# Output projection of an attention block: earlier loads of some heads, and modulation sums moved behind other products

## The chip, the cores and the metric

The kernel runs on one core of one Trainium2 chip. The metric is the time of one execution on the device, in microseconds (us). One execution is also recorded by the hardware profiler; its record is called the trace, and the summary of it the page. All numbers below come from such traces or from timed runs. Two numbers of different sharpness are used: the time of the whole, which differs by 2 us and more from run to run, and the length of one stage in a trace, which repeats to 0.2 us in the kernel before (two traces).

## The reference, cut to what matters

```python
mod = (silu(c) @ w_mod).reshape(1, 6, 1, -1)
sa, ca, ga, sb, cb, gb = mod[:, 0], ..., mod[:, 5]
h = layernorm(x) * (1 + ca) + sa
x = x + ga * attention(h, k_cache, v_cache, wq, wo)      # ends in: concat(heads) @ wo
h = layernorm(x) * (1 + cb) + sb                         # needs sb, cb
x = x + gb * gmlp(h, w_in, w_sp, b_sp, w_out)
```

There are 2048 tokens, width 1024 and 32 heads of 128. The stage in question is `concat(heads) @ wo`, a product of 2048 x 4096 by 4096 x 1024. While it runs, the kernel also computes `sb` and `cb`, which the next layer norm needs: 16 columns of 128 values, each a weighted sum of a slice of `w_mod` with `silu(c)`. These are the modulation sums.

## The kernel before

The projection is cut into eight blocks of 256 tokens. Each block does a 2 x 2 matrix product with seven products in place of eight (the Strassen and Winograd way). A product is 16 matmuls of 128 x 128 by 128 x 512. The price of the saved product is operand sums, which VectorE (DVE) makes: `o_sum`.

Blocks overlap. In the steady state the order of the products is 1 and 2 of block n, 3 of block n-1, 6 and 7 of block n, 4 of block n-1, 5 of block n, and then block n+1. What has to happen behind a product hangs on it as a hook. Reading a finished product out of TensorE's result memory and adding it to x is called its evacuation. In the timelines below, DVE and the queue of loads work through their instructions in the order of the program: the modulation sum at 1246.34 us holds up the evacuation behind it, and a store at 1287.7 us the loads behind it.

```python
SPOTS = ((2, 1), (2, 2), (1, 4), (2, 6), (2, 7), (3, 1), ...)   # (block, product); 28 of them
mod_at = {}
for q in range(16):
    k = q * 8 // 5
    mod_at.setdefault(SPOTS[k + 3], []).insert(0, lambda q=q: mod_sum(q))
    mod_at.setdefault(SPOTS[k], []).append(lambda q=q: load_mod(q))
...
def load_mod(q):                       # a transposing load, 256 KB, two buffers
    t = wm_t[q] = mods.tile([P, D], BF16, name="wm_t", tag="wm_t", bufs=2)
    nc.sync.dma_start(out=t[:], in_=w_mod[:, 3*D + P*q : 3*D + P*(q + 1)], transpose=True)

def load_heads(n, k):                  # block n; pair k=0 feeds products 1 and 7, k=1 feeds 2 and 4
    for q in (2 * k, 2 * k + 1):
        t = oq[n, q] = heap.take("oq", [P, 8, 256], BF16)
        nc.sync.dma_start(t[:, :m, :], oT_dram[8*q : 8*q + m, :, n*256 : (n + 1)*256]...)
...
    for n in range(3, 8):              # the hooks of blocks 3 to 7
        hk = wos[n].hooks
        hk[1] = [o_sum(n, 1), o_sum(n, 3)]     # (lambdas left out)
        hk[2] = [o_sum(n, 2)]                  # product 6 reads this one
        hk[6] = [o_sum(n, 4), ...]             # and product 5 o_sum 1
        ...
        if 4 <= n and n < 8:
            wos[n - 1].on(3 if n < 6 else 4, lambda n=n: n < 7 and load_heads(n + 1, 1))
...
def row_done(ti):                      # both halves of 128 rows of x are finished
    nc.sync.dma_start(x1_dram[ti], x1[:])      # a store that waits for DVE's last add
```

All loads and stores stand in one queue, that of SyncE, in program order. `heap.take` hands out slots of 4 KB per partition, the one that has been free for longest first; a load into a slot waits until the slot's last reader is done.

The softmax here doesn't subtract the row's maximum and nothing guards it: scores larger than these inputs give would overflow.

## Time and profile before

| | before |
|---|---|
| time | 1757.7 us, median of 3 runs (1757.69 to 1757.94) |
| span in the trace | 1754.6 us |
| TensorE (PE) busy | 1734.4 us, 99% |
| DVE busy | 1522.0 us, 87% |
| start of the projection in the trace | 1128.66 us |
| start of the next stage | 1314.33 us |
| **length of the projection** | **185.67 us** |

The two lines of the page that give the busy times of the engines:

```profile
span 1754.6 us, 23657 instructions
PE 1734.4 (99%) x8414; PEld 794.2 (45%) x8414; DVE 1522.0 (87%) x2324; ACT 1298.3 (74%) x1530; POOL 34.1 (2%) x39
```

TensorE is the bound: nothing but its pauses can be won. The Trainium skill (Perfetto Trace Analysis, "Optimization Strategy") advises just that: find the gaps between the slices of the engine that bounds, and what each waits for. The view of waits, for TensorE from 1128 to 1319 us, has three lines (total us, times, longest us):

```profile
PE a L995 <- DVE s_slots L1065: 0.4, 1, 0.4
PE a L995 <- DVE h_slots L1065: 0.3, 1, 0.3
PE c L995 <- DMA wq_t<-oT_dram: 0.3, 1, 0.3
```

This view counts the time between the drawn end of one matmul and the start of the next, and leaves out short ones. The timeline shows more. Its columns are start, duration from first start to last end, engine, line, operation, tiles, shape, number of instructions merged, and in brackets the idle time before with its cause. Here are TensorE's rows of the kernel before: the start of the projection, block 2 (products 1 and 2), block 5 (the second half of product 3 of block 4, then product 6), block 7 (product 1, the halves of product 2, the second half of product 3 of block 6, product 6) and the first row of the next stage:

```profile
1128.66 1.89 PE L995 MATMUL c<-tx,h_slots 128*128 128x512 bf16 x8
...
1170.31 3.62 PE L995 MATMUL a<-wo,oq 128*128 128x512 bf16 x16
1173.92 1.90 PE L995 MATMUL c<-tx,s_slots 128*128 128x512 bf16 x8
1175.75 1.90 PE L995 MATMUL c<-s_slots,oq 128*128 128x512 bf16 x8
...
1248.28 1.89 PE L995 MATMUL a<-s_slots,oq 128*128 128x512 bf16 x8
1250.48 2.76 PE L995 MATMUL a<-h_slots 128*128 128x512 f16 x12 [0.31 <-DVE h_slots L1065]
...
1288.78 3.62 PE L995 MATMUL a<-wo,oq 128*128 128x512 bf16 x16
1292.51 1.90 PE L995 MATMUL c<-tx,h_slots 128*128 128x512 bf16 x8
1294.72 1.90 PE L995 MATMUL c<-s_slots,wq_t 128*128 128x512 bf16 x8 [0.31 <-DMA wq_t<-oT_dram]
...
1298.19 1.89 PE L995 MATMUL a<-s_slots,h_slots 128*128 128x512 bf16 x8
1300.51 2.76 PE L995 MATMUL a<-h_slots,s_slots 128*128 128x512 f16 x12 [0.43 <-DVE s_slots L1065]
...
1314.33 1.49 PE L995 MATMUL a<-h_slots 128*128 128x448 bf16 x7
```

Eight matmuls at full pace take 1.73 us, sixteen take 3.46 us.

What DVE did before product 6 of block 5, in the timeline of the kernel before (L1067 is `o_sum` 3, L933 the modulation sum, L1043 to L1117 the evacuation of product 2, L1065 `o_sum` 2):

```profile
1245.74 0.69 DVE L1067 TENSOR_TENSOR wq_t<-wq_t 128x1024 f16<-128x1024 bf16 x1
1246.34 1.22 DVE L933 SCALAR_TENSOR_TENSOR wm_t<-wm_t,silu_bc 128x1024 bf16<-128x1024 bf16 x1
...
1247.68 0.69 DVE L1043 TENSOR_TENSOR sum<-c,snap 128x512 f32<-128x512 f32 x1
...
1249.74 0.68 DVE L1065 TENSOR_TENSOR h_slots<-os_12192,h_slots 128x1024 f16<-128x1024 f16 x1
```

The modulation sum at 1246.34 stands between the operand sums and the evacuation of product 2, which TensorE had finished before 1247.

The queue of loads and stores around block 7's second head pair (L1084 is the store of x1, L681 a head load; the 11.16 us are two stores merged, the second issued at the end of it):

```profile
1274.62 1.60 SPq L1090 DMA_DIRECT2D h_dram<-hb  x1
1276.86 11.16 SPq L1084 DMA_DIRECT2D x_dram<-x_in  x2
1288.11 0.39 SPq L681 DMA_DIRECT2D h_slots<-oT_dram  x1
1288.59 0.63 SPq L681 DMA_DIRECT2D wq_t<-oT_dram  x1
```

The head loads were not issued until the store ahead of them got its data from DVE, whose last add to x (L1117) ran from 1286.98 to 1287.67 us. They are needed at 1292.2 us.

### The profile page before, as it was taken

Reading aid. Unit: us, or ns where it says so; the run is one execution under the profiler, and the core shown is the slowest. Engines: PE = TensorE matmul, PEld = TensorE weight load, DVE = VectorE, ACT = ScalarE, POOL = GpSimd, SP = SyncE. Lnnn points to the kernel's source line nnn. Section 1 sums busy time; section 2 is a strip of 40 time slices with the busy share of each in tenths; the row PEclk is TensorE's granted clock in tenths of the full one; section 3 lists DMA queues with packets and bytes.
Section 4 is the critical chain, followed back from the end, with each engine's and each line's share of the span. In section 5 each row is a group of like instructions: output and inputs, shape, how many; then the busy total and the mean of one; then the engine's idle time right before and its main releaser. Section 6 shows DMA issues by size and latency. Waiting matters only on the chain.

```text
span 1754.6 us, 23657 instructions
## 1 busy us (share of the span) xinstructions
PE 1734.4 (99%) x8414; PEld 794.2 (45%) x8414; DVE 1522.0 (87%) x2324; ACT 1298.3 (74%) x1530; POOL 34.1 (2%) x39
## 2 busy tenths in 40 slices
PE   7999999999999999999999999999999999999999
PEld 4444444444444444444444444444444444444444
DVE  6898898898988899998999988988879788778975
ACT  7998889999999999999999999711235666737500
POOL 1000000000000000000000000000100000000000
PEclk9999999999999999999999999999999999999999
DMA  8575466645435643555643464658958544548222
GB/s 252 134 186 137 116 148 163 152 127 136 122 94 137 161 103 102 145 151 130 156 120 100 129 183 131 186 128 204 215 165 220 142 122 124 180 119 230 60 78 96
DMA packets 465895, 253.78 MB, mean 145 GB/s; under 512 B 310640, under 2 KB 425584, under 8 KB 465776
## 3 DMA queue, kind: packets, MB, share of 16 engines
q1 hardware_dynamic: 465776, 252.26, 54.0%
q8 instruction: 66, 1.08, 0.3%
q14 instruction: 53, 0.43, 0.1%
HBM read 142.08 MB, written 55.59 MB: 113 GB/s over the span
## 4 chain that ended last, share of the span: by engine, by line
PE 90%; DVE 6%; DMA 2%; ACT 1%; issue 1%; SPq 0%; DVEq 0%; ACTq 0%
PE sps L510 24%; PE ops L787 24%; PE a L995 16%; PE b L995 9%; PE qa L491 4%; PE c L995 4%; PE qps L408 4%; PE qb L491 3%; PE bo L1617 1%; DMA wm<-in_w_mod_dram 1%; ACT pt L850 1%; DVE sum L1043 1%; PE a_11083 L995 1%; DVE stats L155 0%; DMA wq_t<-oT_dram 0%
## 5 line engine op out<-in xcount | busy, mean ns | idle before, releaser
L850 ACT ACTIVATE pt<-sps 128x1024 bf16<-128x1024 f32 x1008 | 1004.3, 1024 | 77.5 <-PE sps L510 35.2
L510 PE MATMUL sps<-qT,kT 128*128 128x512 bf16 x2048 | 609.3, 379 | 2.3 <-ACT pt L850 1.2
L787 PE MATMUL ops<-pt,v_sb 128*128 128x512 bf16 x2048 | 598.9, 379 | 0.0
L510 PEld LDWEIGHTS <-kT 128*128 128x128 bf16 x2048 | 199.6, 98 | 247.3 <-issue 14.5
L787 PEld LDWEIGHTS <-v_sb 128*128 128x128 bf16 x2048 | 200.1, 98 | 243.2 <-issue 1.6
L1038 ACT ACTIVATE snap<-a 128x512 f32<-128x512 f32 (+1 forms) x111 | 60.6, 565 | 103.0 <-PE a L995 84.9
L866 DVE COPY ou<-ops 128x512 f32<-128x512 f32 x126 | 81.1, 685 | 31.2 <-PE ops L787 28.5
L995 PEld LDWEIGHTS <-h_slots 128*128 128x128 f16 (+1 forms) x714 | 69.6, 98 | 84.0 <-DVE h_slots L1065 1.7
L408 PE MATMUL qps<-h1T,wq_t 128*128 128x512 bf16 x288 | 96.7, 379 | 0.0
L1043 DVE TENSOR_TENSOR sum<-b,snap 128x512 f32<-128x512 f32 (+1 forms) x76 | 50.1, 659 | 36.2 <-PE b L995 18.5
L1466 ACT ACTIVATE zr<-zr,z_nm,z_rs 128x256 f16<-128x256 f16 x90 | 45.0, 590 | 41.9 <-DMA zr<-z_dram 41.9
L666 DVE TENSOR_TENSOR oT<-ou,rbc 128x1024 bf16<-128x1024 f32 x62 | 75.3, 1215 | 0.3 <-DMA rbc<-rec_dram 0.3
L476 DVE COPY tx<-qa 128x512 f32<-128x512 f32 x66 | 45.4, 688 | 31.0 <-PE qa L491 30.9
L644 DVE TENSOR_REDUCE den<-pT 128x8 f32<-128x1024 bf16 x58 | 68.6, 1182 | 0.8 <-DMA pT<-sums_dram 0.8
L491 PE MATMUL qa<-h1s,wq_t 128*128 128x512 f16 x176 | 63.1, 379 | 0.0
L995 PEld LDWEIGHTS <-s_slots 128*128 128x128 f16 (+1 forms) x415 | 40.3, 98 | 50.2 <-DVE s_slots L1386 1.5
L149 POOL TENSOR_TENSOR rstd<-var,neg_half 128x1 f32<-128x1 f32 x30 | 28.7, 955 | 1295.2 <-DVE var L147 1250.7
L491 PEld LDWEIGHTS <-wq_t 128*128 128x128 bf16 (+1 forms) x352 | 34.4, 98 | 41.6
L995 PEld LDWEIGHTS <-wq_t 128*128 128x128 f16 (+1 forms) x344 | 33.6, 98 | 39.7 <-DMA wq_t<-oT_dram 0.8
L471 DVE TENSOR_TENSOR qT<-qb,tx 128x512 bf16<-128x512 f32 x66 | 45.2, 684 | 0.8
L408 PEld LDWEIGHTS <-wq_t 128*128 128x128 bf16 x288 | 28.2, 98 | 33.9 <-issue 0.6
L491 PEld LDWEIGHTS <-tx 128*128 128x128 f16 x264 | 25.8, 98 | 31.2
(975 smaller groups left out, 2586.1 us busy)
## 6 DMA issues: line engine op xcount, KB each, us to landing
rbc<-rec_dram SPq DMA_DIRECT2D x63, 512.0 KB
v_sb<-in_A_v_cache_dram SPq DMA_DIRECT2D x40, 512.0 KB
oT_dram<-oT SPq DMA_DIRECT2D x62, 256.0 KB
sums_dram<-pacc SPq DMA_DIRECT2D x58, 256.0 KB
wm<-in_w_mod_dram SPq DMA_DIRECT2D x8, 1024.0 KB
wq_t<-in_A_wq_dram SPq DMA_DIRECT2D x7, 1024.0 KB
zr<-z_dram SPq DMA_DIRECT2D x12, 512.0 KB
h_slots<-oT_dram SPq DMA_DIRECT2D x10, 512.0 KB
```

The source lines that it names most:

```text
L408: nc.tensor.matmul(box["ps"][:], weights[:, dc, hc:hc + DH], src[:, dc, q0:q0 + 512], start=(n == 0), stop=(n == KD - 1))
L476: nc.vector.tensor_copy(out=x if m == 6 else su, in_=a)
L491: nc.tensor.matmul(box["b" if m in (2, 7, 4) else "a"][:], *operand(m, dc), start=(m in (1, 2, 7) and dc == 0), stop=(dc == 3), skip_group ...
L510: nc.tensor.matmul(sps[:, j * 512:(j + 1) * 512], kts[h][:, kb * P:(kb + 1) * P], qts[(h, qh)][:, j * 512:(j + 1) * 512], start=True, stop ...
L644: nc.vector.tensor_reduce(out=den[:], in_=state[i]["pT"][:], op=ALU.add, axis=mybir.AxisListType.X)
L666: nc.vector.tensor_mul(out=oT, in0=state[i]["ou"][:], in1=state[i]["rbc"][:])
L787: nc.tensor.matmul(o_ps[j][:], vs[halves[i][0]][:, kb, :], pt_tiles[g][:, j * 512:(j + 1) * 512], start=(kb == 0), stop=(kb == NKB - 1))
L850: nc.scalar.activation(pt_tiles[g], s_tiles.pop(g)[:], ACT.Exp, scale=SCALE, **bias)
L866: nc.vector.tensor_copy(out=ou[:, j * 512:(j + 1) * 512], in_=o_ps[j][:])
L995: nc.tensor.matmul(self.ps[self.BANK[n]], a, b, start=(n in (1, 2, 7) and k == 0), stop=(k == len(lhs) - 1), skip_group_check=True)
L1038: nc.scalar.activation(t, ps, ACT.Copy)
L1043: nc.vector.tensor_add(out=t, in0=ps, in1=snap)
```

## The change

The intent is to feed the products in time. (1) Heads of blocks 2, 3 and 7 are loaded one to three products sooner. (2) The modulation sums stand only behind products 6, 7 and 5, where DVE's work is not awaited soon; for that, loads of up to three columns are issued at once and there is a third buffer. (3) To make room for it, the row `silu_bc` moves to a shared slot, which shifts every later slot assignment by one.

```diff
-    silu_bc = mods.tile([P, D], BF16, name="silu_bc")
+    silu_bc = heap.take("silu_bc", [P, D], BF16)
...
-        t = wm_t[q] = mods.tile([P, D], BF16, name="wm_t", tag="wm_t", bufs=2)
+        t = wm_t[q] = mods.tile([P, D], BF16, name="wm_t", tag="wm_t", bufs=3)
...
-    SPOTS = ((2, 1), (2, 2), (1, 4), ...)
     mod_at = {}
-    for q in range(16):
-        k = q * 8 // 5
-        mod_at.setdefault(SPOTS[k + 3], []).insert(0, lambda q=q: mod_sum(q))
-        mod_at.setdefault(SPOTS[k], []).append(lambda q=q: load_mod(q))
+    LOADS = {2: ((2, 1), (2, 1), (2, 1), (2, 7)), 3: ((3, 1), (3, 1), (3, 2), (3, 7)),
+             4: ((2, 4), (2, 4), (4, 1), (4, 7)), 5: ((3, 4), (3, 4), (5, 1), (5, 7))}
+    for n in range(2, 6):
+        for k, m in enumerate((6, 7, 7, 5)):
+            q = 4 * (n - 2) + k
+            mod_at.setdefault((n, m), []).append(lambda q=q: mod_sum(q))
+            mod_at.setdefault(LOADS[n][k], []).append(lambda q=q: load_mod(q))
+    mod_at[6, 1] = [lambda: heap.give(silu_bc)]
...
     heap.give(oq[1, 0], oq[1, 1])
+    load_heads(2, 1)
     wos[0].run(3)
...
     heap.give(oq[0, 2], oq[0, 3])
-    load_heads(2, 1)
+    load_heads(3, 0)
     load_x(4)
     load_x(5)
     wos[1].run(3)
     wos[2].run(1)
-    load_heads(3, 0)
...
-            wos[n - 1].on(3 if n < 6 else 4, lambda n=n: n < 7 and load_heads(n + 1, 1))
+            if n < 7:
+                wos[n - (n < 6)].on(3 if n < 6 else 7, lambda n=n: load_heads(n + 1, 1))
```

More of the change, by code (lines that the diff above doesn't have):

```diff
@@ L1124 @@
     wos = [wo_block(n) for n in range(8)]
-    SPOTS = ((2, 1), (2, 2), (1, 4), (2, 6), (2, 7), (3, 1), (2, 5), (3, 2), (2, 3), (3, 6),
-             (3, 7), (2, 4), (3, 5), (4, 1), (4, 2), (3, 3), (4, 6), (4, 7), (3, 4), (4, 5),
-             (5, 1), (5, 2), (4, 3), (5, 6), (5, 7), (4, 4), (5, 5), (6, 1))
     mod_at = {}
-    for q in range(16):
-        k = q * 8 // 5
-        mod_at.setdefault(SPOTS[k + 3], []).insert(0, lambda q=q: mod_sum(q))
-        mod_at.setdefault(SPOTS[k], []).append(lambda q=q: load_mod(q))
+    LOADS = {2: ((2, 1), (2, 1), (2, 1), (2, 7)), 3: ((3, 1), (3, 1), (3, 2), (3, 7)),
[6 more added lines that the diff above has]
+    mod_at[6, 1] = [lambda: heap.give(silu_bc)]
     for (n, m), fns in mod_at.items():
```

## The prediction

> **What bounds it.** TensorE. The page's busy line gives PE 1734.4 us of a 1754.6 us span (99%); the chain that ended last is 90% PE. The output projection (about 1130 to 1319 us) is a row of 16-matmul products, 3.45 us each in the timeline, back to back, fed by DVE, which is 77 to 99% busy in most 10 us stretches. So only gaps between matmuls can be won. The timeline and the waits of PE show five over 50 ns in the projection:
>
> - 1250.2: 0.31 us, product 6 of block 5 waits for DVE's second operand sum
> - 1274.8: 0.13 us, product 6 of block 6, the same wait
> - 1292.4: 0.11 us and 1294.4: 0.31 us, product 2 of block 7 waits for two head loads
> - 1300.1: 0.43 us, product 6 of block 7 waits for a DVE sum pushed back by the same late heads (DVE idles 0.7 and 1.5 us for them)
>
> Sum 1.30 us, 0.07% of the time. Before 1250 there is none.
>
> **What the change does.** No work is added or removed: DVE still runs 16 modulation sums of 1.22 us (+0.08 us accumulator read, +0.15 us in half of them).
>
> 1. Modulation sums move. One at 1246.3 and one at 1270.7 stood between the operand sums behind product 1 and product 2's evacuation, which DVE started 0.9 and 0.6 us late; product 6 paid. In the new DVE order none stands there: both gaps (0.44 us) vanish. Two sums now stack behind product 7 (2.7 us), with three products of slack; counting DVE's work, I find the operand sums done some 0.5 us early.
>
> 2. Block 7's second head pair. Its loads stood in the in-order DMA queue behind an x1 store that waited from 1277 for DVE: issued 1288.1 and 1288.6, landed 4 to 6 us later, too late. Now they are issued ahead of that store, when their slots come free (products 6 and 7 of block 6: 1278.4 and 1280 to 1282), with DMA nearly idle (17% from 1280 to 1290). They land by about 1286, 6 us early: three gaps (0.86 us) vanish. The Trainium skill (Perfetto Trace Analysis, "DMA Instruction — HWDGE") says that an issue's profiled start is when its semaphores are satisfied, so a blocked queue shows as a gap between issues: the trace agrees, over 10 us without one.
>
> 3. Heads of blocks 2 and 3 sooner: DVE waited 1.3 us for one, PE never. Worth 0.
>
> 4. A third modulation buffer, the silu row moved to the shared slots: every later slot assignment moves by one. No load gets a slot whose last reader is later than its need.
>
> **On the critical path.** 1.30 us of PE gaps, about all of it won. The stages behind hold 1.4 us of small gaps (1329 to 1366: waits for ACT and DVE, DVE full) and one of 0.56 us at 1476, which may move a few tenths either way. 1757.7 - 1.3 = 1756.4 us.
>
> **To see.** No such five gaps; block 7's second head pair issued about 1278 to 1282; no modulation sum between product 1's and product 2's DVE work; DVE not waiting for heads in block 7; blocks 2 to 4 still without gaps.
>
> **What would make it wrong.** Three modulation transposes in a row hold up heads queued behind them, or DVE waits for a modulation load that now waits for its buffer: a new PE gap of 1 to 3 us in blocks 3 to 6. Or the gelu stage, where DVE is full, gives the gain back.
>
> Chances: faster by over 2% 0.003, within 2% 0.994, slower 0.003. Range 1755.5 to 1757.5 us.

## The result, and the profile after

| | before | after |
|---|---|---|
| time, median of 4 runs | 1757.82 us (1757.69 to 1758.35) | 1754.94 us (1754.26 to 1755.23) |
| span in the trace | 1754.6 us | 1752.4 us |
| start of the projection | 1128.66 us | 1128.94 us |
| **length of the projection** | **185.67 us** | **183.23 us** |
| next stage, up to the plain output product | 260.54 us | 260.54 us |

The ratio is 0.9982, with a 95% interval of 0.9965 to 1.0: the same within 2%, as forecast, but 2.9 us less where 1.3 us were forecast. A ratio here is the mean time of one kernel's fast runs over that of the other's of the same rounds, so it is not quite the ratio of the medians. The measured time lies 0.56 us below the range forecast. The traced executions, one of each kernel, took 1756.39 and 1754.26 us, 2.1 us apart; so part of the 2.9 us may be chance, which is looked at below.

The trace puts the gain into the projection, 2.44 us shorter, and nowhere behind it. The first line of the page after, and TensorE's rows after that answer to those before. The view of waits of TensorE has no line left for the projection.

```profile
PE 1734.1 (99%) x8414; PEld 795.6 (45%) x8414; DVE 1522.7 (87%) x2324; ACT 1297.7 (74%) x1530; POOL 31.3 (2%) x39
```

```profile
1128.94 1.89 PE L995 MATMUL c<-tx,h_slots 128*128 128x512 bf16 x8
...
1170.58 3.62 PE L995 MATMUL a<-wo,oq 128*128 128x512 bf16 x16
1174.03 1.89 PE L995 MATMUL c<-tx,oq 128*128 128x512 bf16 x8
1175.76 1.89 PE L995 MATMUL c<-s_slots,wq_t 128*128 128x512 bf16 x8
...
1248.28 1.89 PE L995 MATMUL a<-s_slots,oq 128*128 128x512 bf16 x8
1250.00 2.75 PE L995 MATMUL a<-h_slots 128*128 128x512 f16 x12
...
1291.44 1.89 PE L995 MATMUL c<-tx,oq 128*128 128x512 bf16 x8
1293.17 1.89 PE L995 MATMUL c<-s_slots,wq_t 128*128 128x512 bf16 x8
...
1296.62 1.89 PE L995 MATMUL a<-s_slots,h_slots 128*128 128x512 bf16 x8
1298.35 2.75 PE L995 MATMUL a<-h_slots,wq_t 128*128 128x512 f16 x12
...
1312.16 1.68 PE L995 MATMUL a<-wq_t,hT 128*128 128x448 bf16 x8
```

Now every eight matmuls take 1.72 or 1.73 us from start to start. PE's busy time is the same as before (1734.1 against 1734.4 us), although the kernel is faster: a drawn matmul lasts 379 ns whether or not the next one is on time.

DVE after: the evacuation of product 2 follows `o_sum` directly, and even waits 0.40 us for TensorE. The queue after: the second head pair of block 7 is issued at 1278.69 and 1279.34, ahead of the store that now ends at 1286.91.

```profile
1245.73 0.69 DVE L1067 TENSOR_TENSOR wq_t<-wq_t 128x1024 f16<-128x1024 bf16 x1
1246.82 0.69 DVE L1043 TENSOR_TENSOR sum<-c,snap 128x512 f32<-128x512 f32 x1 [0.40 <-PE c L995]
...
1248.88 0.68 DVE L1065 TENSOR_TENSOR h_slots<-h_slots,oq 128x1024 f16<-128x1024 f16 x1
```

```profile
1275.82 0.33 SPq L1084 DMA_DIRECT2D x_dram<-x_in  x1
1278.69 0.37 SPq L681 DMA_DIRECT2D oq<-oT_dram  x1
1279.34 0.37 SPq L681 DMA_DIRECT2D wq_t<-oT_dram  x1
1286.91 0.33 SPq L1084 DMA_DIRECT2D x_dram<-x_in  x1
```

So both mechanisms show in the traces as predicted, and the size does not. Reading the stalls of the kernel before once more, now as the distance of two matmul starts less 216 ns:

| stall at (us) | what waits | by drawn gaps | by starts | difference |
|---|---|---|---|---|
| 1173.5 | product 2 of block 2, first head load | none | 0.16 | 0.16 |
| 1175.4 | the same, second head load | none | 0.09 | 0.09 |
| 1249.8 | product 6 of block 5, `o_sum` 2 | 0.31 | 0.48 | 0.16 |
| 1274.4 | product 6 of block 6, `o_sum` 2 | 0.13 | 0.29 | 0.16 |
| 1292.0 | product 2 of block 7, first head load | 0.11 | 0.28 | 0.16 |
| 1294.0 | the same, second head load | 0.31 | 0.48 | 0.16 |
| 1299.7 | product 6 of block 7, `o_sum` 2 | 0.43 | 0.60 | 0.16 |
| sum | | 1.30 | 2.37 | |

The difference of 0.163 us, the same at all five drawn stalls, is 379 - 216 ns: in these traces a matmul of 128x512 is drawn for 379 ns but the next starts after 216. If so, a pause of less than 163 ns is not drawn at all, and any longer one is drawn 163 ns too short. This is the pace theory. Its rivals: the gap theory of the prediction (1.30 us from these stalls), with the rest from another cause, such as the shifted slots or the third buffer, or from the spread of the runs.

### The profile page after: what moved, and what is told of

Read it like the earlier page. It is cut to its first block, busy times and chain, and to the rows that moved or that the text cites. A ratio compares the mean times of both kernels' runs of the same rounds, so it can differ in the third digit from the quotient of the medians.

```text
span 1752.4 us, 23647 instructions
## 1 busy us (share of the span) xinstructions
PE 1734.1 (99%) x8414; PEld 795.6 (45%) x8414; DVE 1522.7 (87%) x2324; ACT 1297.7 (74%) x1530; POOL 31.3 (2%) x39
## 4 chain that ended last, share of the span: by engine, by line
PE 93%; DVE 4%; DMA 1%; ACT 1%; issue 1%; SPq 0%; DVEq 0%; ACTq 0%
PE sps L510 24%; PE ops L787 24%; PE a L995 17%; PE b L995 9%; PE c L995 4%; PE qa L491 4%; PE qps L408 4%; PE qb L491 3%; PE bo L1619 1%; ACT pt L850 1%; DMA wm<-in_w_mod_dram 1%; PE a_11083 L995 1%; DVE sum L1043 0%; DVE stats L155 0%; PE a L1717 0%
## 5 line engine op out<-in xcount | busy, mean ns | idle before, releaser
L995 PEld LDWEIGHTS <-h_slots 128*128 128x128 f16 (+1 forms) x756 | 73.9, 98 | 87.5 <-issue 1.4
L995 PEld LDWEIGHTS <-wq_t 128*128 128x128 f16 (+1 forms) x390 | 38.1, 98 | 45.1 <-issue 0.3
L995 PEld LDWEIGHTS <-s_slots 128*128 128x128 f16 (+1 forms) x363 | 35.4, 98 | 43.3 <-DVE s_slots L1388 1.5
```

What stands on the lines that cost most here:

```text
L995: nc.tensor.matmul(self.ps[self.BANK[n]], a, b, start=(n in (1, 2, 7) and k == 0), stop=(k == len(lhs) - 1), skip_group_check=True)
```

## The experiments

The measure in all of them is the length of the projection, from the start of its first row to the first 448-wide row, and the stalls in it by starts (those over 20 ns). A summary first:

| kernel | projection (us) | stalls of block 2 | of blocks 5 and 6 | of block 7 |
|---|---|---|---|---|
| before | 185.67 | 0.25 | 0.77 | 1.35 |
| before2 | 185.51 | 0.36 | 0.78 | 1.09 |
| b_layout | 185.16 | 0.47 | 0.72 | 0.69 |
| b_heads23 | 184.94 | 0 | 0.77 | 0.88 |
| b_mods | 184.39 | 0.39 | 0 | 0.74 |
| b_heads7 | 184.29 | 0.27 | 0.76 | 0 |
| after, after2, after3, and the four g_ kernels | 183.23 | 0 | 0 | 0 |
| a_heads3back | 183.23 | 0 | 0 | 0 |
| a_probe | 183.38 | 0.13 in blocks 4 and 5 together, put in on purpose | | |
| a_twobuf | 195.32 | other stalls, below | | |

### One part alone: b_heads7, b_heads23, b_mods, b_layout

`b_heads7` is the kernel before with block 7's part:

```diff
-            wos[n - 1].on(3 if n < 6 else 4, lambda n=n: n < 7 and load_heads(n + 1, 1))
+            if n < 7:
+                wos[n - (n < 6)].on(3 if n < 6 else 7, lambda n=n: load_heads(n + 1, 1))
```

> The kernel before with one part alone: block 7's second head pair loaded behind product 7 of block 6. Measure: length of the projection, from the start of its first product to the start of the first 448-wide matmul, 185.67 us before and 183.23 us after. Pace theory (a stall costs the distance of two matmul starts less the pace of 216 ns): the stalls of block 7 before were 0.28, 0.48 and 0.60 us, so the length falls by 1.35 to 184.32 us. Gap theory (a stall costs the gap between one matmul's drawn end and the next start, as in the prediction): it falls by 0.86 to 184.81 us. Other-cause theory (the shifted slots or the third buffer won the surplus): as the gap theory. Heads issued near 1278 to 1282 us, stalls of blocks 2, 5 and 6 unchanged.

Measured: 184.29 us, 1.38 less, as the pace theory has it (184.32) and not as the gap theory has it (184.81). The loads were issued at 1281.42 and 1281.88 in a trace whose projection began 1.7 us later than that of before. All three stalls of block 7 were gone, those of blocks 2, 5 and 6 were there still. The ratio of the whole was 1.0003 (0.9986 to 1.002): the total can't show 1.4 us here, since the seven runs of before beside it spread from 1754.76 to 1758.69 us.

`b_heads23` is the kernel before with the earlier loads of blocks 2 and 3:

```diff
     heap.give(oq[1, 0], oq[1, 1])
+    load_heads(2, 1)
...
-    load_heads(2, 1)
+    load_heads(3, 0)
...
     wos[2].run(1)
-    load_heads(3, 0)
```

> The kernel before with one part alone: heads of blocks 2 and 3 loaded sooner. Pace theory: block 2's product 2 was stalled by 0.16 and 0.09 us although no gap was drawn (375 and 308 ns between starts against 216), so the projection falls by 0.25 to 185.42 us. Gap theory: 0, so 185.67 us. Stalls of blocks 5, 6 and 7 unchanged.

Measured: 184.94 us, 0.73 less; more than either theory. Block 2's two stalls, which were never drawn, are gone, which the gap theory has no place for. The other half of a microsecond comes from block 7, whose stalls were 0.88 us in this trace instead of 1.35. The ratio of the whole was 0.9996 (0.9981 to 1.001).

`b_mods` is the kernel before with the new places of the modulation sums and loads, the third buffer and the row in the shared slot; all head loads are where they were. Its edit is the first three parts of the diff above.

> The kernel before with one part alone: modulation sums behind products 6, 7 and 5, with the third buffer and the silu row in the shared slots that it needs; head loads as before. Pace theory: the stalls of 0.48 us in block 5 and 0.29 us in block 6 vanish, so the projection falls by 0.77 to 184.90 us. Gap theory: by 0.44 to 185.23 us. Block 7's three stalls stay; block 2's may change by a tenth, as more transposes are queued near them.

Measured: 184.39 us, 1.28 less. The stalls of blocks 5 and 6 are gone, by starts as well. Block 7's fell to 0.74 and block 2's rose to 0.39, neither of which I had expected in that size. The ratio was 1.0 (0.9985 to 1.0015).

`b_layout` is the kernel before with the third buffer and the shared slot alone:

```diff
-    silu_bc = mods.tile([P, D], BF16, name="silu_bc")
+    silu_bc = heap.take("silu_bc", [P, D], BF16)
...
-        t = wm_t[q] = mods.tile([P, D], BF16, name="wm_t", tag="wm_t", bufs=2)
+        t = wm_t[q] = mods.tile([P, D], BF16, name="wm_t", tag="wm_t", bufs=3)
...
+    mod_at[6, 1].append(lambda: heap.give(silu_bc))
```

> The kernel before with only the third modulation buffer and the silu row in the shared slots (freed behind product 1 of block 6); sums and loads in their old places. Pace and gap theory: no change within 0.1 us, 185.67 us, all seven stalls still there. Other-cause theory: the surplus of about 1.1 us over the prediction appears here.

Measured: 185.16 us, 0.51 less; a miss of my "within 0.1". The stalls of blocks 5 and 6 stayed (0.47 and 0.25). Block 2's grew to 0.47 and block 7's fell to 0.69. So the shifted slots may do something, but they are not the surplus of 1.1 us: blocks 2, 5 and 6 stalled by 1.19 us in all, no less than before, and the full change has no late head load left. `b_mods`, with the same slots, had 0.74 us in block 7. Both lie below the 0.88 to 1.35 us of the three traces with the old slots and block 7's old order (before, before2, b_heads23), as does DVE's wait for block 7's second head load (0.77 and 0.78 us against 1.09 to 1.52). That points to the slots; why, the traces don't show. The ratio was 1.0009 (0.9994 to 1.0023).

The parts taken alone win 1.38, 0.73 and 1.28 us, 3.39 together, while the whole wins 2.44: `b_heads23` and `b_mods` also had shorter stalls in block 7 than the first trace (0.88 and 0.74 us against 1.35), which their edits were not meant to give. Counted by the stalls that each one removes by design, they win 1.35, 0.25 and 0.77 us, together 2.37.

### How far the stage repeats: before2, after2

> The kernel before once more, to see how far a profile of the projection repeats. If the stage is set by the program, its length is 185.67 us again within 0.1 us, with the same seven stalls; if the landing of head loads varies from run to run, block 2's and block 7's stalls (0.25 and 1.35 us in the first profile) differ by some tenths and those of blocks 5 and 6 (DVE order: 0.48 and 0.29 us) do not.

Measured: 185.51 us. The DVE stalls repeat (0.48 and 0.30 us), the head stalls don't quite: block 2 0.36 instead of 0.25, block 7 1.09 instead of 1.35. The change therefore saves 2.28 to 2.44 us of the projection, by these two traces of before. They come from different calls, and the calls ran on several chips (7, 1 and 13 for those on record), so run and chip can't be told apart here.

> The changed kernel once more with five rounds against the kernel before. Pace theory: the projection is 183.23 us within 0.05 us and no two matmul starts in it are over 236 ns apart; the whole is 2.0 to 2.9 us faster. Gap theory: 1.3 us faster.

Measured: 183.23 us again, with no pause over 20 ns between matmuls. The totals in these five rounds: mean 1755.71 us against 1756.73 of nine runs of before, ratio 0.9992 (0.9978 to 1.0005). So 1.0 us, less than the stage says, and the interval holds both. The total was not what I had expected.

### A pause that is not drawn: a_probe

If the pace theory is right, a DVE delay of the right size must cost time without a gap in the drawing. The probe is an idle reduction behind product 1 of blocks 4 and 5 of the changed kernel; its result is not used.

```diff
+    def probe(n):
+        den = small.tile([P, 8], FP32, name="den", tag="den")
+        nc.vector.tensor_reduce(out=den[:, 0:1], in_=silu_bc[:, 0:n], op=ALU.add,
+                                axis=mybir.AxisListType.X)
+    wos[4].probe, wos[5].probe = 1024, 832
+    for n in (4, 5):
+        mod_at.setdefault((n, 1), []).append(lambda n=n: probe(wos[n].probe))
```

> The changed kernel with one idle DVE reduction behind product 1 of block 4 (1024 columns, about 1.15 us) and of block 5 (832 columns, about 0.94 us), sized so that product 6 of each block comes late by less than the 163 ns by which a drawn matmul (379 ns) overlaps the next start (216 ns). DVE's idle time there is 0.58 and 0.40 us and product 6 had some 0.38 us to spare, so about 0.19 and 0.16 us are lost. Pace theory: the projection grows by 0.35 (0.2 to 0.5) to about 183.58 us although hardly a gap is drawn. Gap theory: drawn gaps of at most 0.03 us, so no growth over 0.05 us.

Measured: 183.38 us, 0.15 more, which is less than the 0.2 to 0.5 expected; product 6 came less late than I had estimated. The eight traces of the changed projection without a probe gave 183.23 us, so the 0.15 us are clear of the spread. The kind of the effect is as the pace theory says and not as the gap theory says. The rows of `a_probe` around product 6 of blocks 4 and 5, and the probe on DVE:

```profile
1223.34 1.89 PE L995 MATMUL a<-s_slots,h_slots 128*128 128x512 bf16 x8
1225.13 2.76 PE L995 MATMUL a<-h_slots 128*128 128x512 f16 x12
...
1247.59 1.89 PE L995 MATMUL a<-s_slots,oq 128*128 128x512 bf16 x8
1249.38 2.76 PE L995 MATMUL a<-h_slots 128*128 128x512 f16 x12
```

```profile
1221.21 1.21 DVE L1138 TENSOR_REDUCE den<-silu_bc 128x1 f32<-128x1024 bf16 x1
```

The distances are 1.79 and 1.79 us instead of 1.73. The stalls are 73 and 59 ns. In the drawing, the matmul before overlaps the late one by 90 and 104 ns, no bracket stands there, and the view of waits has no line. The time was lost all the same.

### Is the third buffer needed: a_twobuf

```diff
-        t = wm_t[q] = mods.tile([P, D], BF16, name="wm_t", tag="wm_t", bufs=3)
+        t = wm_t[q] = mods.tile([P, D], BF16, name="wm_t", tag="wm_t", bufs=2)
```

> The changed kernel with two modulation buffers instead of three: the third load of block 2 then waits for the first sum, and holds up the queue. If the third buffer is needed, the second head pair of block 3 is issued at about 1190 us rather than 1184 and block 3's product 2 stalls by 0.5 to 2 us; if not, the projection stays at 183.23 us.

Measured: 195.32 us, 12.1 us more than the changed kernel (one run: 1767.79 us). The buffer is needed, but not for the reason that I gave. The heads of block 3 were late as foreseen (issued 1190.64 and 1191.31), but its product 2 did not stall. DVE did: it waited for modulation columns whose loads had waited for their buffer. The view of waits for DVE, 1165 to 1330 us, then one of TensorE's rows:

```profile
DVE wm_t L933 <- DMA wm_t<-in_w_mod_dram: 13.2, 6, 5.0
```

```profile
1280.24 1.89 PE L995 MATMUL a<-s_slots,wq_t 128*128 128x512 bf16 x8
1286.15 1.44 PE L995 MATMUL a<-h_slots,os 128*128 128x512 f16 x4 [4.02 <-DVE os L1065]
```

Three times product 6 came late, by 2.1, 2.6 and 4.2 us. After the last two, TensorE ran at half pace (427 ns from start to start) for 3.2 and 3.6 us, which cost another 3.2 us together; the granted clock was 0.52 from 1256 to 1259.5 us and 0.59 from 1286 to 1290.2 us. This is the one trace with a lower granted clock in the projection (0.98 from 1120 to 1330 us). It is also the danger that the prediction named ("DVE waits for a modulation load that now waits for its buffer"), kept away by the third buffer.

### Which of the two early head pairs: a_heads3back

```diff
     heap.give(oq[0, 2], oq[0, 3])
-    load_heads(3, 0)
...
     wos[2].run(1)
+    load_heads(3, 0)
```

> The changed kernel with only block 3's first head pair back in its old place, behind product 1 of block 2. If block 3's earlier load is worth something by itself, block 2's or 3's products stall by over 0.1 us; if only block 2's is (my view: block 3 had no stall before the change), the projection stays at 183.23 us within 0.1 us.

Measured: 183.23 us without a stall. Block 3's earlier load is worth nothing by itself; block 2's is worth what its two undrawn stalls cost.

### A try at going further: g_tasks, g_act, g_both, g_act5

The stage behind the projection lost 3.1 us in stalls, by starts, in the kernel before and in the changed one. `g_tasks` queues the last eight sums of the spatial weights later; `g_act` gives one slice of four of the second modulation of h to ScalarE (ACT); `g_both` has both edits, and `g_act5` is `g_act` timed with five rounds. The edit of `g_act`, then that of `g_tasks`:

```diff
-            if c == 0:
+            if c == 0 or dc == 3:
                 nc.scalar.activation(t[:, dc, :], t[:, dc, :], ACT.Identity, ...)
```

```diff
-    z2b[15].on(4, ..., lambda: tasks.extend(sums[8:]), lambda: after(7, lambda: (
-        z2_norms(), ...
+    z2b[15].on(4, ..., lambda: after(7, lambda: (
+        tasks.extend(sums[8:]), z2_norms(), ...
```

> A try to beat both kernels, in the next stage, which is 260.54 us long in every profile so far, 3.1 us of it stalls: the changed kernel with the last eight of the sums of the spatial weights queued seven products later, so that DVE does the gelu weights' sums in time at 1471 to 1476 us. The stalls of 0.14 and 0.73 us there vanish if DVE's order is their cause: the stage falls to 259.7 us. A miss if the sums then come late elsewhere.

Measured: 260.95 us, a miss. The stalls of 0.14 and 0.73 us vanished, and a new one of 1.31 us came at 1484.8 us, where another of the sums is late.

> Second try: the changed kernel with a quarter of the second modulation of h (one slice of four) on ACT instead of DVE, about 1.4 us less for DVE and 2.9 us more for ACT between 1338 and 1353 us. If DVE's load is the cause of the stalls of 0.37, 0.83 and 0.29 us at 1352 to 1363, they shrink by over half and the stage falls by about 0.8 us to 259.7 us; if ACT is as full, they stay or grow.

Measured: 259.56 us, 0.98 us less, a little better than expected. The stall of 0.37 us is gone and that of 0.83 us is 0.22; the one of 0.29 us stayed. The rows of `after` and then of `g_act` there:

```profile
1352.71 0.92 PE L995 MATMUL b<-s_slots,h_slots 128*128 128x448 f16 x4 [0.20 <-DVE sum L1043]
1354.29 1.02 PE L995 MATMUL a<-tx,h_slots 128*128 128x512 f16 x4 [0.66 <-ACT snap L1038]
```

```profile
1354.83 0.92 PE L995 MATMUL b<-s_slots,h_slots 128*128 128x448 f16 x4
1355.81 1.02 PE L995 MATMUL a<-tx,h_slots 128*128 128x512 f16 x4
```

> Both tries together, with five rounds. If both work, the stage behind the projection falls to about 258.9 us and the whole is about 1.6 us below the changed kernel, so 3 to 4.5 us below the kernel before; totals vary by some 2 us from run to run, so the stage's length in the profile decides.

Measured: 260.00 us, so `g_tasks` takes back nearly half (0.44 us) of what `g_act` wins (0.98). Five runs had a mean of 1754.72 us against 1757.31 of nine of before, ratio 0.9984 (0.9971 to 0.9998).

> The changed kernel with one of four slices of the second modulation of h on ACT, timed. The stage behind the projection was 259.56 us in one look against 260.54; so about 1.0 us below the changed kernel of the same call and about 3.4 us below the kernel before, if the totals' spread of 2 us lets it be seen. Stage 259.56 us again within 0.05 us.

Measured: 259.57 us again; mean 1754.47 us against 1757.46, ratio 0.9983 (0.9971 to 0.9996). The changed kernel in the same call had 1755.00 us. The lead of 0.5 us in the totals is inside the spread; the shorter stage, seen twice, is not.

### Is the total's surplus real: after3

> The changed kernel, five more rounds on one chip. If the surplus is spread, the mean difference to the kernel before lies between 1 and 3.5 us and its average over the three comparisons near 2.4 us; if it is a real part outside the projection, near or over 2.9 us here too. Projection 183.23 us again, the attention stage before it as long as in profiles of the kernel before with the same granted clock.

Measured: 183.23 us; mean 1755.00 us against 1757.46, ratio 0.9988 (0.9974 to 1.0002). The three comparisons of the changed kernel give differences of the means of 3.08, 1.02 and 2.45 us, on average 2.2 us, which is the projection's 2.28 to 2.44 us within the spread. Over all, the 14 timed runs of the changed kernel and the 38 of the kernel before have means of 1755.21 and 1757.26 us, 2.05 us apart. So the first comparison was, as far as these runs tell, a favourable draw.

Much of the spread lies before the projection. It starts anywhere from 1128.2 to 1131.8 us in the traces of the kernels here, and this goes for the most part with the granted clock from 15 to 30 us. The view by windows of 15 to 30 us, of `after3` and then of `after2`, the same program (columns: window, its length, busy time and count of PE, PEld, DVE, ACT, POOL, granted clock, DMA share, GB/s):

```profile
15.00:30.00 15.00, 12.90 (x227) 9.25 (x224) 8.17 (x27) 9.64 (x14) 1.54 (x3) 1.00 1.18 355
```

```profile
15.00:30.00 15.00, 13.06 (x180) 9.92 (x177) 6.78 (x21) 7.88 (x11) 1.58 (x3) 0.77 1.23 360
```

At 1.00 the projection began at 1128.3 us, at 0.77 at 1131.5 us, with 180 instead of 227 matmuls done in these 15 us. The clock is not all of it: `a_heads3back` had 1.00 there too, but 205 matmuls, and began at 1130.1 us; why, was not looked into.

## Why the prediction was wrong, point by point

- **Bound, and where the gain is: right.** The gain is in the projection alone; the stages behind stayed at 260.54 us.
- **"Sum 1.30 us": the failed step.** The term was mis-sized. The seven stalls cost 2.37 us, measured from start to start, and removing them shortened the projection by 2.28 to 2.44 us. I had read the drawn gaps, which are 163 ns short at each stall. The Trainium skill warns of this (Perfetto Trace Analysis, "Tensor Engine Instruction (MATMUL, LD_WEIGHTS)"): the end of a matmul in the profile is estimated from the size of the instruction, not observed. This trace agrees: 379 ns drawn, 216 ns pace. `a_probe` shows the case in which nothing is drawn and time is lost.
- **1, the modulation sums: mechanism right, size 0.44 predicted, 0.77 measured.** `b_mods` removed the two stalls and no others by design. None of the stacked sums behind product 7 came too late.
- **2, block 7's heads: mechanism right, size 0.86 predicted, 1.35 by the stalls of the first trace and 1.38 in `b_heads7`** (1.09 by the second trace of before). The loads were issued at 1278.7 and 1279.3, as forecast or sooner.
- **3, heads of blocks 2 and 3 "worth 0": wrong for block 2.** "PE never" waited in the drawing, but it lost 0.25 us, and 0.27 to 0.47 us in the other traces with block 2's old order. Right for block 3.
- **4, slots: right for the full change.** With late heads still there, block 7 stalled some tenths less (`b_layout`, `b_mods`); why, stays open.
- **The range was too narrow, too.** It rested on three runs that spread by 0.25 us. Over all sets, 38 runs of the kernel before spread from 1754.76 to 1759.16 us. With the right sum the prediction would have been 1757.7 - 2.4 = 1755.3 us, 0.4 us from the measured 1754.94 us, which is less than that spread.

## What to carry to other kernels

On TensorE, measure a stall as the distance between two matmul starts less the steady pace of that shape, never as the space between a drawn end and the next start: in these traces, short stalls vanished in the drawing, and each of the others was too short by the overlap. When a change is worth a few microseconds in a thousand, judge it by the length of its stage in several traces, and set the range of the total by many runs, not by three. Look for loads that stand behind a store in the same queue: here they waited for the store's data (issued at 1288.1 us, against 1278.7 when moved ahead of it), and moving them ahead cost nothing that the trace shows, as their slots came free in time.

## What the Trainium skill lacked or had wrong

- Perfetto Trace Analysis, "Identifying the Most-Contended Engine", says that pipelined PE instructions look smaller in the trace. Here they look larger, 379 ns drawn against a pace of 216 ns, so that busy time stays at 99% and 1734 us with and without 2.4 us of stalls. Its warning that the busy share of matmuls is no good measure is borne out all the same. The advice in "Optimization Strategy" to find the gaps between slices lacks the warning that on TensorE a gap can be drawn too short (163 ns here, at 128x512) and a stall below that not at all.
- TensorE: Matmul & The Clock Gate, "Back-to-back issue gap", gives about 131 ns per matmul at N=512 for a stream of weight loads and matmuls, and about 216 ns for the isolated gap. Thousands of such pairs in these traces ran at 215 or 216 ns and none of the projection's faster, so the smaller figure did not hold here, and the larger one held for a stream too.
- The same page ("HAM oscillation") gives as a rule that pauses of TensorE should not exceed about 3.4 us. In `a_twobuf` a pause of 2.6 us was followed by half pace (427 ns from start to start) for 3.2 us, one of 2.1 us was not. One trace can't show what parts the two.
